# All instructions in the main block instead of a block per engine with an all-engine barrier at its end

## The chip, the cores and the metric

The kernel runs on one core of one Trainium2 chip. The trace shows five engines of the core, each with its own row of instructions: TensorE (PE in the profile), VectorE (DVE), ScalarE (ACT), GpSimd (POOL) and SyncE (SP). In this kernel they wait for one another through semaphores. For transfers between device memory and the core's on-chip memory the page gives each queue's share of 16 DMA engines; of the 83 issues in the trace of the kernel before, 81 are SP's and 2 ACT's.

The metric is the device time of one execution in microseconds (us). Each run also lists the core's *span*: from the first to the last recorded instruction of the program. The two are not the same (time less span was 1.25 to 1.88 us in the runs of this study), and the difference between them turns out to matter here.

## The reference, cut to what matters

```python
def reference(A_x, A_k_cache, A_v_cache, A_wq, A_wo, B_x, B_W_gate, B_W_up, B_W_down, gate_w):
    g = sigmoid((A_x * gate_w).sum(-1))
    a = attention(A_x, A_k_cache, A_v_cache, A_wq, A_wo)   # one token, 16 query heads,
                                                           # 8 key/value heads, 65536 keys of 256
    b = gated_mlp(A_x, B_W_gate, B_W_up, B_W_down)         # 448 -> 1792 -> 448
    return g * a + (1 - g) * b                             # (1, 1, 448)
```

The two caches are 8 x 65536 x 256 bfloat16 each, 268 MB. Every byte is used once for one token, so the work is reading memory: 549.03 MB by the page of the kernel before, at 428 GB/s over the span.

## The kernel before

The kernel collects its operations in a plan. Each operation has an engine, a sort key, a function that emits its instructions, and the operations that it depends on. `emit` writes one engine's operations in order, with a wait ahead of each where needed:

```python
    def emit(self, e, prog, eng):
        seen = {}
        for o in prog:
            need = {}
            for d in o.deps:
                k = ("d", d.dma) if d.dma is not None else ("e", d.eng)
                need[k] = max(need.get(k, 0), d.count)
            for k, v in need.items():
                if seen.get(k, 0) < v:
                    seen[k] = v
                    eng.wait_ge(self.dsem[k[1]] if k[0] == "d" else self.esem[k[1]], v)
            ins = o.fn(eng)
            ...                                   # increments the engine's or the DMA's semaphore
```

SP issues first the weights of the query projection, then the other weights and the K and V tiles of 8 MB, into a ring of three buffers. VectorE transposes each K tile, TensorE computes scores and later the weighted sum of V, ScalarE the exponentials. The end is a chain: last piece of V, TensorE, VectorE, TensorE's last projection, two copies, the output's transfer.

```python
        f0 = op("dv", T_END, lambda e: e.tensor_copy(fin_o[:, 0:D2], A_ps[0:1, 0:D2]), [fin])
        f1 = op("ac", T_END, lambda e: e.copy(fin_o[:, D2:D], A_ps[32:33, 0:D2]), [fin])
        f2 = dma("sp", T_END + 1, "out", lambda e: e.dma_start(out[0, :, :], fin_o), [f0, f1])
        ...
        progs = pl.finish()

        block = es.enter_context(nc.Block())

        @block.sync
        def _(e):
            pl.emit("sp", progs["sp"], e)
            e.wait_ge(pl.dsem["out"], 16)

        @block.tensor
        def _(e):
            pl.emit("pe", progs["pe"], e)
        ...                                       # vector, scalar, gpsimd alike
```

`nc.Block()` gives each engine a block of its own. The main block then ends with one branch per engine into these blocks, each of them ends with a branch to a common end, and at the common end stands an all-engine barrier: four engines drain (an instruction of that name, which by its record adds to a semaphore), GpSimd drains too, waits for all four and releases them. Another barrier of the same kind stands at the very start of the program, after four constants that GpSimd fills (MEMSETs from 0.24 to 0.43 us). It comes from the construction of the program and is in both kernels.

Of the kernel before, what the change touches and what calls it, by code (L numbers as in the profile page):

```python
# [90 lines left out]
def bass_gated_mix__gqa_block_cached__glu_gated_reglu__decode_kernel(  # L91
# [34 lines left out]
    es = ExitStack()  # L126
    with es:
# [62 lines left out]
        pl = _Plan(nc, es)  # L190
# [362 lines left out]
        pl.serialize(touch_m)  # L553
        progs = pl.finish()

        block = es.enter_context(nc.Block())

        @block.sync
        def _(e):
            pl.emit("sp", progs["sp"], e)  # L560
            e.wait_ge(pl.dsem["out"], 16)

        @block.tensor
        def _(e):
            pl.emit("pe", progs["pe"], e)

        @block.vector
        def _(e):
            pl.emit("dv", progs["dv"], e)

        @block.scalar
        def _(e):
            pl.emit("ac", progs["ac"], e)

        @block.gpsimd
        def _(e):
            pl.emit("gp", progs["gp"], e)

    return nc

# [27 lines left out]
```

## Time and profile before

| | before |
|---|---|
| time, median of 3 runs (range) | 1284.43 us (1284.39 to 1284.6) |
| span of the profiled run | 1283.3 us |
| moved from memory | 549.67 MB, mean 428 GB/s |
| busy: VectorE, TensorE | 49%, 33% |
| start of SP's first load | 0.72 us |
| start of the output's issue | 1281.73 us |

From the page of the kernel before: the span, the share of DMA time in 40 equal slices (a 9 is 90% or more), and the main queue (packets, MB, share of the 16 engines' span).

```profile
span 1283.3 us, 9919 instructions
...
DMA  9999999999999999999999999999999999999997
...
q1 hardware_dynamic: 12930, 549.03, 99.2%
```

Three stretches of the same run. The columns are: stretch, length, busy time of the five engines, granted clock, DMA share, GB/s.

```profile
0.00:40.00 40.00, 11.74 (x79) 8.95 (x80) 16.31 (x38) 1.86 (x3) 4.09 (x21) 0.81 0.96 403
40.00:1237.00 1197.00, 397.79 (x4319) 147.80 (x4323) 616.06 (x381) 59.33 (x112) 0.00 (x0) 0.62 1.00 433
1237.00:1283.30 46.30, 17.45 (x208) 6.15 (x200) 1.23 (x3) 0.34 (x1) 0.00 (x0) 0.68 0.82 335
```

The DMA engines are full for 1197 us. Nothing that the change touches happens there. What can be gained lies before the first load is issued and after the last bytes have landed. The beginning, from the timeline (start, duration, engine, line, operation; "q" marks an engine's sequencer):

```profile
0.33 0.10 POOL L593 MEMSET const-uint8-127<- 128x1 uint8 x1
0.72 0.51 ACTq L236 DMA_DIRECT2D P_sb<-in_A_x_dram  x1
0.72 0.39 SPq L407 DMA_DIRECT2D ring<-in_A_wq_dram  x1
0.78 0.06 DVE L239 MEMSET one_t<- 1x1 bf16 x1 [0.78 <-PEq L593]
```

The end, from the timeline, and then from the waits of SP's queue (who waited for whom, us in total, times, longest):

```profile
1281.31 0.38 DVE L549 CAST P_sb<-A_ps 1x224 bf16<-1x224 f32 x1 [1.51 <-PE A_ps L358]
1281.73 0.32 SPq L551 DMA_DIRECT2D out_dram<-P_sb  x1
```

```profile
SPq L127 <- DMA out_dram<-P_sb: 0.8, 1, 0.8
SPq L593 <- PEq L593: 0.7, 1, 0.7
SPq L127 <- PEq L127: 0.2, 1, 0.2
```

L127 is the line of the context that the block closes with. SP waits there for the output's landing and then, in the barrier, for the other engines.

### The profile page before, as it was taken

What the parts mean: (1) busy time and instruction counts of PE and PEld (TensorE: products, weight loads), DVE (VectorE), ACT (ScalarE), POOL (GpSimd) and SP (SyncE); (2) the same over time, 40 slices, a digit from 0 to 9 for tenths busy, and PEclk for the clock granted to TensorE, in tenths of its full rate; (3) what the DMA queues carried; (4) which work ended last, traced back from release to release, by engine and by line L of the source; (5) the groups of instructions that cost most, each with busy time, mean ns of one, the idle gap of its engine ahead of it and who ended that gap; (6) DMA issues with size and microseconds to landing.
All of it is one profiled execution on the core that took longest, in us unless ns stands there. A gap on an engine that the chain in (4) does not pass through costs nothing.

```text
span 1283.3 us, 9919 instructions
## 1 busy us (share of the span) xinstructions
PE 427.0 (33%) x4600; PEld 162.9 (13%) x4600; DVE 633.6 (49%) x421; ACT 61.5 (5%) x116; POOL 4.1 (0%) x21
## 2 busy tenths in 40 slices
PE   3633332334123432224331243321433323233235
PEld 2401110111001210001110111100111101011111
DVE  2597633465533655434555444555434555335600
ACT  0000000000000000000000000000000000000000
POOL 1000000000000000000000000000000000000000
PEclk8656666656666565667665666655666656666567
DMA  9999999999999999999999999999999999999997
GB/s 398 431 436 432 432 437 432 432 434 432 436 427 436 434 434 429 432 436 434 429 432 437 434 434 432 436 427 432 435 438 425 432 440 434 430 427 440 431 408 313
DMA packets 12975, 549.67 MB, mean 428 GB/s; under 512 B 1283, under 2 KB 3590, under 8 KB 3974
## 3 DMA queue, kind: packets, MB, share of 16 engines
q1 hardware_dynamic: 12930, 549.03, 99.2%
q8 instruction: 36, 0.59, 0.2%
q14 instruction: 5, 0.04, 0.0%
q10 hardware_dynamic: 4, 0.00, 0.0%
HBM read 549.03 MB, written 0.00 MB: 428 GB/s over the span
## 4 chain that ended last, share of the span: by engine, by line
DVE 34%; DMA 32%; another core or an unknown queue 16%; PE 15%; SPq 1%; ACT 1%; issue 1%
DVE ring L335 30%; DMA ring<-in_A_k_cache_dram 27%; PE ST L347 7%; PE O L378 6%; DMA ring<-in_B_W_up_dram 3%; DMA ring<-in_A_wo_dram 2%; DVE P_sb L480 1%; SPq L521 1%; DVE nmb L458 1%; PE PT L485 1%; PE M_ps L429 1%; PE M_ps L432 0%; ACT ptp L494 0%; DVE o_sb L389 0%
## 5 line engine op out<-in xcount | busy, mean ns | idle before, releaser
L335 DVE STREAM_TRANSPOSE ring<-ring 128x2048 uint32<-128x2048 uint32 x256 | 565.4, 2275 | 410.0 <-DMA ring<-in_A_k_cache_dram 410.0
L347 PE MATMUL ST<-ring,xm 128*16 128x512 bf16 x2048 | 224.2, 612 | 755.2 <-DVE ring L335 755.2
L347 PEld LDWEIGHTS ST<-ring,xm 128*16 128x16 bf16 x2048 | 61.9, 120 | 903.0 <-DVE ring L335 794.6
L378 PE MATMUL O<-ring,ptp 128*4 128x512 bf16 x2048 | 149.0, 453 | 34.3 <-DMA ring<-in_A_v_cache_dram 30.3
L460 ACT ACTIVATE P_sb<-ST,nmb 128x512 bf16<-128x512 f32 x32 | 45.3, 1414 | 1112.7 <-DVE nmb L458 1112.7
L458 DVE TENSOR_REDUCE nmb<-ST 128x1 f32<-128x512 f32 x32 | 22.0, 689 | 110.7 <-PE ST L347 110.7
L378 PEld LDWEIGHTS O<-ring,ptp 128*4 128x4 bf16 x2048 | 54.5, 99 | 128.5 <-issue 58.3
L389 DVE CAST o_sb<-O 128x512 bf16<-128x512 f32 x8 | 5.5, 692 | 80.5 <-PE O L378 80.5
L480 DVE TENSOR_TENSOR P_sb<-P_sb,hs 128x1024 bf16<-128x1024 bf16 x16 | 18.9, 1222 | 8.7 <-ACT hs L474 8.7
L485 PE MATMUL PT<-identb,P_sb 128*128 128x128 bf16 x128 | 16.6, 310 | 15.5 <-DVE P_sb L480 14.7
L429 PE MATMUL M_ps<-xT,ring 128*128 128x1 bf16 x84 | 9.4, 205 | 16.3 <-DMA ring<-in_B_W_up_dram 16.3
L485 PEld LDWEIGHTS PT<-identb,P_sb 128*128 128x128 bf16 x128 | 12.3, 140 | 18.3 <-DVE P_sb L480 18.3
L494 ACT COPY ptp<-PT 128x256 bf16<-128x256 bf16 x32 | 10.3, 375 | 23.0 <-PE PT L485 23.0
L307 PE MATMUL M_ps<-ring,P_sb 128*128 128x256 bf16 x64 | 10.1, 335 | 3.2 <-DMA ring<-in_A_wq_dram 3.2
L429 PEld LDWEIGHTS M_ps<-xT,ring 128*128 128x128 bf16 x84 | 7.2, 151 | 16.9 <-issue 16.5
L460 ACT ACTIVATION_READ_ACCUMULATOR P_sb<-ST,nmb 128x1 f32 x32 | 8.5, 267 | 0.0
L307 PEld LDWEIGHTS M_ps<-ring,P_sb 128*128 128x128 bf16 x64 | 7.6, 120 | 5.5 <-issue 3.3
L432 PE MATMUL M_ps<-xT,ring 128*64 128x1 bf16 x56 | 7.8, 276 | 0.0
L412 DVE STREAM_TRANSPOSE ptp<-P_sb 128x128 uint32<-128x128 uint32 x1 | 0.3, 313 | 13.5 <-ACT P_sb L411 13.5
L470 PE MATMUL M_ps<-identf,hs 128*2 128x128 f32 x8 | 2.6, 321 | 10.0 <-DVE hs L468 10.0
L432 PEld LDWEIGHTS M_ps<-xT,ring 128*64 128x64 bf16 x56 | 5.4, 191 | 0.4
L358 PE MATMUL A_ps<-ring,attnT 128*1 128x224 bf16 x64 | 4.6, 305 | 2.5 <-DMA ring<-in_A_wo_dram 2.5
(72 smaller groups left out, 60.1 us busy)
## 6 DMA issues: line engine op xcount, KB each, us to landing
ring<-in_A_v_cache_dram SPq DMA_DIRECT2D x1, 4096.0 KB, 29.3
ring<-in_A_wq_dram SPq DMA_DIRECT2D x1, 3072.0 KB, 10.2
ring<-in_A_wo_dram SPq DMA_DIRECT2D x1, 2240.0 KB, 31.8
ring<-in_A_v_cache_dram SPq DMA_DIRECT2D x1, 2048.0 KB, 23.6
ring<-in_B_W_down_dram SPq DMA_DIRECT2D x1, 1568.0 KB, 20.6
ring<-in_B_W_gate_dram SPq DMA_DIRECT2D x1, 1344.0 KB, 32.6
ring<-in_B_W_up_dram SPq DMA_DIRECT2D x1, 1344.0 KB, 35.3
ring<-in_A_v_cache_dram SPq DMA_DIRECT2D x1, 1024.0 KB, 25.6
```

What stands on the lines that cost most here:

```text
L307: ins = e.matmul(QN_ps, xw3[:, k_, 31 - j:159 - j], rhs, start=(j == 0 and kt == 0), stop=(j == J - 1 and kt == R3))
L335: return lambda e: e.transpose(v, v)
L347: ins = e.matmul(bank[32 * w:32 * w + 16, :], xm[:, x0:x0 + 16], ktv[sl][:, u0:u0 + 16, c, :, r_], start=(b == 0 and c == 0 and r_ == 0), ...
L378: ins = e.matmul(OP[h % 2][32 * g:32 * g + 4, :], ptp[h % 2][:, col:col + 13:4], ring[sl][:, k * 512:(k + 1) * 512], start=(a == 0 and k < ...
L429: e.matmul(GU_ps[:, c:c + 1], wf3[which][:, kt * F + ft:(kt + 1) * F:FT], xT[:, kt:kt + 1], start=(kt == 0), stop=False, skip_group_check= ...
L432: ins = e.matmul(GU_ps[64 * half:64 * half + 64, c:c + 1], wfh[which][:, ft:F // 2:FT], xT[:, R3 + half:R3 + half + 1], start=False, stop= ...
L458: smax[n] = op("dv", tk + 22, lambda e, n=n, NM=NM, t_=t_: e.tensor_reduce(NM[:, t_:t_ + 1], ST[n % 2][:], AX.X, ALU.max, negate=True), [q ...
L460: aexp[n] = op("ac", tk + 23, lambda e, n=n, t_=t_, NM=NM, RS=RS: e.activation(P_sb[:, t_:2048:4], ST[n % 2][:], ACTF.Exp, bias=NM[:, t_:t ...
L480: rsc = op("dv", tt, lambda e, X=X, pb=pb: e.tensor_tensor(pb, pb, X[:, 12:16].unsqueeze(1).to_broadcast([128, 256, 4]), ALU.mult), [h7, a ...
L485: ins = e.transpose(PT[rd][:, s * 128:(s + 1) * 128], P_sb[:, (rd * 8 + s) * 128:(rd * 8 + s + 1) * 128], identb[:, :])
L494: ins = e.copy(dst, src)
L521: dep = dma("sp", t, "vp%d" % i, lambda e, sl=sl, n=n, lo=lo, hi=hi: e.dma_start(ring[sl][:, lo * 256:hi * 256], v_src(n)[:, lo * 256:hi * ...
```

## The change

The intent is to save the branch into each engine's block at the start and the barrier at the end. Every engine's instructions are emitted into the main block; the waits between operations stay as they were.

```diff
-        block = es.enter_context(nc.Block())
-
-        @block.sync
-        def _(e):
-            pl.emit("sp", progs["sp"], e)
-            e.wait_ge(pl.dsem["out"], 16)
-
-        @block.tensor
-        def _(e):
-            pl.emit("pe", progs["pe"], e)
-        ...
+        pl.emit("ac", progs["ac"], nc.scalar)
+        pl.emit("sp", progs["sp"], nc.sync)
+        nc.sync.wait_ge(pl.dsem["out"], 16)
+        pl.emit("pe", progs["pe"], nc.tensor)
+        pl.emit("dv", progs["dv"], nc.vector)
+        pl.emit("gp", progs["gp"], nc.gpsimd)
```

More of the change, by code (lines that the diff above doesn't have):

```diff
@@ L554, in bass_gated_mix__gqa_block_cached__glu_gated_reglu__decode_kernel @@
         progs = pl.finish()
-        block = es.enter_context(nc.Block())
-        @block.sync
-        def _(e):
-            pl.emit("sp", progs["sp"], e)
-            e.wait_ge(pl.dsem["out"], 16)
-        @block.tensor
-        def _(e):
-            pl.emit("pe", progs["pe"], e)
-        @block.vector
-        def _(e):
-            pl.emit("dv", progs["dv"], e)
-        @block.scalar
-        def _(e):
-            pl.emit("ac", progs["ac"], e)
-        @block.gpsimd
-        def _(e):
-            pl.emit("gp", progs["gp"], e)
+        pl.emit("ac", progs["ac"], nc.scalar)
[4 more added lines that the diff above has]
+        pl.emit("gp", progs["gp"], nc.gpsimd)
     return nc
```

## The prediction

> **What bounds the kernel now.** The page's DMA row is 9 tenths in every slice but the last, and the queue table puts 99.2% of the 16 engines' span on the hardware queue. From 40 to 1237 us the DMA share is 1.00 at 433 GB/s; in the first 40 us it is 0.96 at 403 GB/s, in the last 46.3 us 0.82 at 335 GB/s. 549.67 MB at 433 GB/s are 1269 us (an estimate from those two numbers) of the 1283.3 us span. The time is the byte stream plus what precedes its first issue and follows its last landing; only those ends can be touched.
>
> **What the change removes.** No operation, transfer, or order within an engine.
> 1. Entry: one branch per engine. The timeline shows the last constant fill on POOL ending at about 0.43 us, the first SP issue at 0.72, the first ACT issue at 0.72, VectorE at 0.78, POOL at 0.82. The 0.3 us between hold the opening barrier, which stays, and the branch, which goes. [...]
> 2. Exit: the all-engine barrier. The output's issue starts at 1281.73 us and takes 0.32; the waits of SP show 0.8 us for the output's landing and then 0.2 us for TensorE's sequencer at the line of the block's exit. Landing is therefore at about 1282.85, and the span ends at 1283.3: 0.45 us are drain and barrier, on the critical path. In the changed kernel only SP's wait for the output is left.
>
> **What it adds or moves.** Nothing. The activation-table load (1.28 us at 1.50 us, on ACT behind its two small loads) could move ahead of those loads; their users have slack: xw is ready at 5.9 us, while the first projection waits for wq until 12.2 us. Should the table load land before the opening barrier, the whole program would start about 1.3 us later; unlikely, as it now stands just before its first user.
>
> **Sum.** [...] None of it is hidden; the run-to-run spread is 0.2 us. The DMA stream may lie a little differently, worth a few tenths to 1 us either way.
>
> Predicted 1283.9 us, 1282.3 to 1285.2 eight times in ten; faster by over 2%: 0.01, within 2%: 0.98, slower by over 2%: 0.01.
>
> **What would show it.** [...] Exit: the span ends at most 0.1 us after the output's landing instead of 0.45; no wait at the exit line for another engine's sequencer. Middle: DMA share 1.00 and 433 GB/s from 40 to 1237 us, K-tile transposes (17.7 us for eight) and busy times unchanged.
>
> **What would make it wrong.** The time measured may not contain the end barrier, or the closing work around the program may take its place [...]; a table load or instruction fetch that starts the stream later by 1 to 2 us; [...] a different memory rate of the stream.

The sum came to about 0.55 us (1284.43 less 0.55 is the 1283.9 us forecast). Of it 0.45 us are the exit; the rest was the entry. It was an estimate for a branch ahead of SP's first load, which was to start a little earlier than at 0.72 us; no trace showed what it rested on. That the stream may differ by a few tenths to 1 us was a guess; in one series of nine runs of the kernel before (that of the first experiments) the spans are 1282.0 to 1284.2 us.

## The result, and the profile after

| | before | after |
|---|---|---|
| time, median of 4 runs (range) | 1284.51 us (1284.39 to 1285.15) | 1284.11 us (1283.34 to 1284.89) |
| ratio of fast runs, 95% interval | | 0.9995 (0.9981 to 1.0009) |
| span of the profiled run | 1283.3 us | 1282.0 us |
| SP's first load | 0.72 us | 0.72 us |
| output's issue | 1281.73 us | 1280.89 us |
| from the output's issue to the end of the span | 1.53 us | 1.16 us |

A ratio is the mean time of one kernel's fast runs over that of the other's of the same rounds, so it is not quite the ratio of the medians. By this comparison the two are the same: 0.4 us between the medians, with single runs 1.5 us apart.

The page of the changed kernel, and its three stretches:

```profile
span 1282.0 us, 9908 instructions
...
DMA  9999999999999999999999999999999999999998
...
q1 hardware_dynamic: 12930, 549.03, 99.4%
```

```profile
0.00:40.00 40.00, 11.52 (x77) 8.74 (x77) 16.10 (x38) 1.86 (x3) 4.09 (x21) 0.82 0.96 403
40.00:1237.00 1197.00, 398.32 (x4317) 147.25 (x4321) 616.26 (x381) 59.33 (x112) 0.00 (x0) 0.61 1.00 433
1237.00:1282.00 45.00, 18.44 (x212) 6.27 (x204) 1.23 (x3) 0.34 (x1) 0.00 (x0) 0.65 0.85 348
```

The middle is the same to the last digit of rate. The start:

```profile
0.72 0.51 ACTq L236 DMA_DIRECT2D P_sb<-in_A_x_dram  x1
0.72 0.40 SPq L407 DMA_DIRECT2D ring<-in_A_wq_dram  x1
0.78 0.06 DVE L239 MEMSET one_t<- 1x1 bf16 x1 [0.78 <-PEq L577]
```

Nothing moved. The end, and the waits of SP:

```profile
1280.46 0.38 DVE L549 CAST P_sb<-A_ps 1x224 bf16<-1x224 f32 x1 [1.51 <-PE A_ps L358]
1280.89 0.32 SPq L551 DMA_DIRECT2D out_dram<-P_sb  x1
```

```profile
SPq L558 <- DMA out_dram<-P_sb: 0.8, 1, 0.8
SPq L577 <- PEq L577: 0.7, 1, 0.7
```

The wait for the other engines is gone, and the page counts 11 instructions fewer. Eleven is just the size of the barrier: a drain and a wait on four engines, a drain and two semaphore instructions on GpSimd. The ten branches of the kernel before are not in that number. The trace's own records, which also hold what the page does not count as busy, show only one of them: SP's closing branch, which carries the wait for the output. In the changed kernel that wait is an instruction of its own, so the count there is even. These are the records after the output's issue, in ns from its start (start, duration):

```
before:  SP branch, waits for the output      1139   33
         SP drain                             1312    7
         GpSimd waits for the four            1344   17
         GpSimd releases them                 1423   17
         SP released                          1464   17
         TensorE released                     1476   51     end of the span: 1527
after:   SP waits for the output              1141   17     end of the span: 1158
```

At the start, SP's first load begins 65 ns after the opening barrier has let SP go in the kernel before (release recorded 11721 to 11738, load at 11803) and 68 ns after it in the changed kernel (11907 to 11924, 11992). Between 65 and 68 ns there is no room left for a branch that takes time.

So the profile shows 0.37 us gained at the end of the span (1.53 less 1.16) and nothing at its start. The profiled spans differ by 1.2 us; the other 0.84 us is the output's issue coming earlier in that run. Whether that is chance or belongs to the kernel was the first question for experiments.

### The profile page after: what moved, and what is told of

It is laid out like the page before. It is cut to its first block, busy times and chain, and to the rows that moved or that the text cites. A ratio compares the mean times of both kernels' runs of the same rounds, so it can differ in the third digit from the quotient of the medians.

```text
span 1282.0 us, 9908 instructions
## 1 busy us (share of the span) xinstructions
PE 428.3 (33%) x4600; PEld 162.3 (13%) x4600; DVE 633.6 (49%) x421; ACT 61.5 (5%) x116; POOL 4.1 (0%) x21
## 4 chain that ended last, share of the span: by engine, by line
DVE 34%; DMA 32%; another core or an unknown queue 16%; PE 15%; SPq 1%; ACT 1%; issue 1%
DVE ring L335 30%; DMA ring<-in_A_k_cache_dram 27%; PE ST L347 7%; PE O L378 6%; DMA ring<-in_B_W_up_dram 3%; DMA ring<-in_A_wo_dram 2%; DVE P_sb L480 1%; SPq L521 1%; DVE nmb L458 1%; PE PT L485 1%; PE M_ps L429 1%; PE M_ps L432 0%; ACT ptp L494 0%; DVE o_sb L389 0%
## 5 line engine op out<-in xcount | busy, mean ns | idle before, releaser
L494 ACT COPY ptp<-PT 128x256 bf16<-128x256 bf16 x32 | 10.3, 375 | 23.0 <-PE PT L485 23.0
```

The costliest lines, as they stand in the source:

```text
L494: ins = e.copy(dst, src)
```

## The experiments

Two quantities are read from each run. The *tail* runs from the start of the output's issue to the end of the span, from the trace of the profiled run. What lies *outside* is a run's time less its span, which every run lists. All kernels computed the right result.

**The changed kernel, more rounds** (no edit).

> The changed kernel once more, with more rounds, to set its gain against the spread. Theory A (the closing barrier lies on the critical path and is all that was gained): 0.3 to 0.5 us under the kernel before, with an interval that may include 0, as single runs differ by 0.7 us or more. Rival B (the gain of the first comparison, 1.2 us in the profiled spans, is real and also comes from a stream that runs better in this kernel): 1 us or more under the kernel before, with an interval clear of 0. Rival C (nothing is gained): 0.0. Tail, from the start of the output's issue to the end of the span: 1.16 us, as in the first profile of it; before 1.53.

Measured: median 1283.95 us against 1285.00 us, ratio 0.9994 (0.9982 to 1.0007), tail 1.16 us. The means are 0.83 us apart (1284.94 and 1284.11), more than theory A's 0.3 to 0.5 and less than rival B's 1 us, with an interval that includes no difference. This decides nothing by itself.

**The barrier put back, without blocks.**

```diff
         pl.emit("gp", progs["gp"], nc.gpsimd)
+        nc.all_engine_barrier()
```

> The changed kernel with one all-engine barrier put back at its end, no branches. Theory A: the tail goes from 1.16 to about 1.5 us (before 1.53), first SP issue stays at 0.72 us, time within 0.2 us of the kernel before. Rival D (the branches into and out of the blocks are part of the gain): tail clearly under 1.5, say 1.35, [...].

Measured: median 1285.02 us, ratio 1.0002 (0.9989 to 1.0014), first load at 0.72 us, tail 1.41 us. The barrier accounts for 0.25 us of the 0.37 us. So theory A's 1.5 us was missed, and rival D is right about the exit and wrong about the entry. In the waits of SP the one for the other engines is back, behind the one for the output:

```profile
SPq L558 <- DMA out_dram<-P_sb: 0.8, 1, 0.8
...
SPq L563 <- PEq L563: 0.2, 1, 0.2
```

The missing 0.12 us stands in the records: here SP's drain begins 56 ns after the wait for the output (1140 to 1196), in the kernel before 173 ns after its branch (1139 to 1312). So with the closing branch, which is recorded, SP's next instruction comes 117 ns later.

**Blocks put back, without the barrier.**

```diff
+        for k, et, e in parts:                      # sp, pe, dv, ac, gp
+            nc.br("blk_" + k, engines=[et])
+        for k, et, e in parts:
+            with nc.body("blk_" + k, valid_engines=[et]):
+                pl.emit(k, progs[k], e)
+                if k == "sp":
+                    e.wait_ge(pl.dsem["out"], 16)
+                nc.br("fin", engines=[et])
+        nc.switch_bb("fin")
```

> The changed kernel with a block per engine put back, written with branches in and out, but no barrier at the end. Theory A: tail 1.16 to 1.2 us, first SP issue at 0.72 us; no record of an entry branch; time as the changed kernel (0.3 to 0.5 us under before). Rival D: [...] a tail of 1.3 us and more.

Measured: median 1284.66 us, ratio 0.9997 (0.9985 to 1.001), first load at 0.72 us, tail 1.17 us. Of ten branches only SP's last is recorded (33 ns, it carries the wait). The branches are 0.01 us of the tail when nothing follows them, as theory A expected. Barrier alone 0.25, closing branch alone 0.01, both 0.37 us: the 0.12 us is the branch ahead of a barrier.

**The barrier ahead of the wait for the output.**

```diff
-        nc.sync.wait_ge(pl.dsem["out"], 16)
         ...
         pl.emit("gp", progs["gp"], nc.gpsimd)
+        nc.all_engine_barrier()
+        nc.sync.wait_ge(pl.dsem["out"], 16)
```

> The changed kernel with the barrier put back, but ahead of SP's wait for the output instead of after it. Theory A says that the barrier costs because it begins after the landing; begun at the output's issue it runs under the 0.8 us of the landing: tail 1.16 to 1.2 us, time as the changed kernel. Rival E (the barrier's work costs wherever it stands, for instance through the longer end of each engine's program): tail about 1.5 us.

Measured: median 1283.94 us, ratio 0.9993 (0.998 to 1.0007), tail 1.15 us. The barrier is done 749 ns after the start of the output's issue, the landing comes at 1133 ns, and SP's waits show both side by side:

```profile
SPq L563 <- DMA out_dram<-P_sb: 0.4, 1, 0.4
SPq L562 <- PEq L562: 0.2, 1, 0.2
```

The barrier took the same 0.2 us of waiting, but out of the landing's time, so it added nothing to the span. Theory A's reason holds for the span, rival E falls.

**32 barriers at the end, and 32 at the start.**

```diff
+        for _ in range(32):                         # start32: here; end32: after the last emit
+            nc.all_engine_barrier()
         pl.emit("ac", progs["ac"], nc.scalar)
```

> 32 all-engine barriers at the end of the changed kernel. Theory A with 0.37 us for the first and somewhat less for those that follow (0.2 to 0.35 us each, a guess from the 0.36 us that drain, gather and release took in before): tail 8 to 12 us, and a time longer than the kernel before by 7 to 11 us, equal to the growth of the tail within 1 us. Rival C (the time measured does not contain the closing barrier): the tail grows in the trace but the time stays within 1 us of before.

> 32 all-engine barriers ahead of the program. If the head is on the critical path as the prediction said, SP's first issue moves from 0.72 us to 8 to 12 us, and the time grows by the same amount within 1 us. Rival F (the head has slack, the stream of bytes catches up): the first issue moves and the time grows by less than half of that.

Measured at the end: tail 12.34 us, which is 1.16 for the landing, 0.25 for the first barrier and (12.34 - 1.41) / 31 = 0.35 us for each further one, in all a little over the 8 to 12 us expected; time 1296.0 us median, mean 11.0 us over the kernel before, for a tail that is 10.8 us longer (12.34 against 1.53). Measured at the start: first load at 11.97 instead of 0.72 us, mean time 10.3 us over the kernel before. (The intervals, 1.007 to 1.0104 and 1.0065 to 1.0095, are clear of 1.)

```profile
11.97 0.38 SPq L407 DMA_DIRECT2D ring<-in_A_wq_dram  x1
```

Both ends pass into the time in full, so rivals C and F fall. There is no slack at the head: what delays the first load passes into the time. (The entry term of the prediction would be too little to see in the time, with runs of the kernel before 0.76 us apart; that the branches into the blocks cost nothing is read from the start of the first load.) What the start misses (11.25 us later, only 10.3 us longer) fits what is found further down: this kernel has no closing barrier, so it begins with an advantage of 0.9 us.

**Branches that really run.** In the first kernel, SP's first seven loads are put into a block each and laid out in reverse. In the second, only the first two stand behind the rest.

```diff
+        nc.br("sp0", engines=[ET.SP])               # taken8
+        for i in reversed(range(8)):
+            with nc.body("sp%d" % i, valid_engines=[ET.SP]):
+                if i < 7:
+                    pl.emit("sp", progs["sp"][i:i + 1], nc.sync)
+                    nc.br("sp%d" % (i + 1), engines=[ET.SP])
+                else: ...                           # the rest of SP's program
```

> SP's first seven loads each in a block of its own, the blocks laid out in reverse, so that eight branches between them cannot be left out by any layout. Tells what a taken branch costs that does run. [...] Time: within 1 us of before either way, as the queue already holds work by then.

Measured: median 1286.25 us, mean 1.13 us over the kernel before, a little outside the 1 us expected. All eight branches are recorded, 33 ns each, under the name COMPARE_BRANCH, which every recorded branch of this study has. The first load starts at 1.18 us instead of 0.72, 461 ns after the start of the branch that leads to it, and its issue takes 2.17 us instead of 0.40; the second starts at 3.56 us. The seventh starts 2.49 us later than in the changed kernel (6.35 against 3.86 us; the seven starts there are 0.72, 1.19, 1.65, 2.12, 2.83, 3.38 and 3.86), and nearly all of it comes from the first jump. From the third to the seventh load, four branches later, 2.26 us pass; in three profiles of the changed kernel 2.21, 2.26 and 2.13 us, and 2.06 us in that of end1, which has no branches either. The records show why so little is left: from the end of one issue to the start of the next 0.20 us pass with a branch between and 0.04 to 0.05 us without, so a short branch takes about 0.16 us of SP's time; but the issues themselves are shorter here, 0.33 to 0.43 us for the third to sixth against 0.42 to 0.67 us in the changed kernel. Together that is lost in the spread between profiles, while the first jump cost over 2 us (0.46 us in the start of the first load and 1.77 us in its issue).

> SP's first two loads laid out behind the rest of its program: one branch forward over 81 instructions, one back. In the run with eight such branches the first issue was 0.45 us late, the second waited 1.8 us longer, and the others came 0.07 us further apart than without branches. If the long waits come from a place that was not yet fetched: first issue about 0.45 us late and 1.5 to 2 us between the second load and the third. If they came from something else in that layout: all issues within 0.15 us of the changed kernel's.

Measured: median 1286.40 us, mean 1.21 us over the kernel before. SP's lines of the timeline:

```profile
1.18 2.10 SPq L407 DMA_DIRECT2D ring<-in_A_wq_dram  x1
3.33 0.41 SPq L408 DMA_DIRECT2D ring<-in_A_wq_dram  x1
4.05 0.32 SPq L452 DMA_DIRECT2D ring<-in_A_k_cache_dram  x1
```

The first issue is again 0.45 us late and again takes 2.1 us, here with a second load right behind it in the same block. The branch back to the third load, however, cost 0.26 us from its start (3.79) and not the 1.5 to 2 us expected. So the expectation was half right: the cost belongs to the first jump, not to each jump. (The first is also the only one among the loads that goes forward; the later ones there go back. The 0.07 us per branch that this text of expectations quotes from the run before is not borne out by the count above.)

The trace also records DMA packets of a kind that it calls "instruction". They would fit a fetch that holds up the long issue, but do not show it (in the changed kernel, SP's issue at 478.57 us lies inside the time of one of 16384 bytes and lasts only 0.33 us). In both kernels one such packet of 8192 bytes lies inside the long issue (from 1.74 us for 0.50 us, and from 1.73 us for 0.47 us); no other kernel has one in the first 6 us. In start32, ACT's first issue takes 1.94 us instead of 0.51 with two such packets inside it, and there is no branch at all. The trace does not say for which engine a packet is, and why SP's issue goes on for another 1.1 us after its packet stays open.

**A branch to a far place.** TensorE's last group of matmuls is laid out at the front of its program.

```diff
+        with nc.body("peb", valid_engines=[ET.PE]):
+            pl.emit("pe", progs["pe"][-1:], nc.tensor)
+            nc.br("fin", engines=[ET.PE])
+        with nc.body("pea", valid_engines=[ET.PE]):
+            pl.emit("pe", progs["pe"][:-1], nc.tensor)
+            nc.br("peb", engines=[ET.PE])
```

> TensorE's last group of projection matmuls (4 matmuls on the chain at the end) laid out at the front of its program, so that its last branch goes back over some 9000 instructions. Tells what a branch to a far place costs. If it stalls for a fetch, TensorE's last four matmuls start 1 to 3 us later after the ones before them than in the changed kernel (there 0.16 us after), and the time grows by 1 to 3 us less what the wait for the last projection weights covers. If not, under 0.2 us.

Measured: median 1288.12 us, mean 2.6 us over the kernel before (one of the four runs, 1285.95 us, was 2 us under the rest). The trace records the branch back with a duration of 3.27 us, from 1281.26 us; its beginning lies under matmuls that still run, and in the chain that ended last 2.71 us of it show as "issue", time in which TensorE waited for nothing that the profile shows:

```profile
1280.68 1.30 PE A_ps L358 x12
1281.98 2.71 issue
1284.70 0.55 PE A_ps L358 x4
```

The last four matmuls begin 3.12 us after the start of the one before them, in the changed kernel 0.23 us (not the 0.16 us of the expectation): 2.9 us later, within the 1 to 3 us expected of a fetch (a guess). The profiles' pages count the packets of the queue that they call "instruction", 16384 bytes each, first of the kernel before, then of this one:

```profile
q8 instruction: 36, 0.59, 0.2%
q8 instruction: 38, 0.62, 0.2%
```

One of the two packets more runs from 1282.22 to 1283.18 us, within the branch, the other from 1285.29 us, after TensorE's last branch to the end. So a branch can be dear: this one, with its target some 9000 instructions back, took 2.7 us on the critical chain, with an instruction packet of 0.96 us inside it. None of the ten in the kernel before is of this kind.

**The surplus, once more** (all three are kernels shown above; no new edit).

> The changed kernel a third time, on whatever chip this is, to separate two readings of the 0.5 to 0.8 us by which its means lay under the kernel before so far. Theory A: the tail is 0.37 us shorter and the rest, the time of the output's issue, differs by chance: mean 0.37 us under before, give or take 0.4, and no steady order among these kernels except by tail. Rival B (the stream itself runs better in this kernel, by about 0.8 us): mean 1.2 us under before.

> The kernel with one barrier put back, again. Its tail was 1.41 us, its mean 0.15 us over before. Theory A: mean 0.12 us under before, give or take 0.4, and 0.25 us over the changed kernel. Rival B: 0.8 to 1 us over the changed kernel, as in the first runs.

> The kernel with the barrier ahead of the wait, again. Its tail was 1.15 us, its mean 1.0 us under before and 1.2 us under the kernel with the barrier at the end, while the tails explain 0.38 and 0.26. Theory A (the surplus was chance): 0.38 us under before and 0.26 us under the kernel with the barrier at the end, give or take 0.4. Rival B: again 1 us and 1.2 us.

Measured, on another chip: changed kernel median 1284.14 us, ratio 0.9992 (0.9979 to 1.0004), mean 1.08 us under the kernel before. Barrier at the end: 1285.23 us, ratio 0.9999, mean 0.16 us under. Barrier ahead of the wait: 1284.07 us, ratio 0.9992, mean 1.00 us under. The two groups of the first series came back (barrier last, and not last), and the surplus with them. Theory A as stated is too small, and chance is no longer a good answer. But rival B's reason is wrong as well. The table takes the mean time of each kernel apart: the output's issue is the mean span less the tail, and outside is the mean of time less span.

| kernel | chip | runs | mean time | output's issue | tail | outside |
|---|---|---|---|---|---|---|
| before | first | 9 | 1284.94 | 1281.62 | 1.53 | 1.80 |
| after_again | first | 5 | 1284.11 | 1281.66 | 1.16 | 1.29 |
| branch_only | first | 5 | 1284.53 | 1281.97 | 1.17 | 1.39 |
| bar_then_wait | first | 5 | 1283.91 | 1281.35 | 1.15 | 1.41 |
| end1 | first | 5 | 1285.10 | 1281.85 | 1.41 | 1.84 |
| before | third | 9 | 1285.25 | 1281.92 | 1.53 | 1.81 |
| after3 | third | 5 | 1284.18 | 1281.71 | 1.15 | 1.32 |
| btw_b | third | 5 | 1284.25 | 1281.68 | 1.16 | 1.41 |
| end1_b | third | 5 | 1285.10 | 1281.87 | 1.41 | 1.82 |
| before | second | 7 | 1285.09 | 1281.79 | 1.53 | 1.78 |
| end32 | second | 4 | 1296.14 | 1282.04 | 12.34 | 1.76 |
| start32 | second | 4 | 1295.43 | 1292.97 | 1.15 | 1.31 |

(The tail of before is that of its one profile. Spans are on record to 0.1 us, so one run's outside is good to 0.05 us.) The stream of bytes runs alike: the output's issue of the changed kernel lies 0.04 us later on one chip and 0.21 us earlier on the other, and kernels without a steady reason differ by as much. Rival B falls: its 0.8 us are not there on either chip. What differs steadily stands in the last column: every kernel whose last act is a barrier has 1.76 to 1.84 us outside its span, every other one 1.29 to 1.41 us (the three kernels with jumping branches, which are not in the table, 1.38 to 1.45 us). Over all 25 runs of before it is 1.74 to 1.86, over all 14 runs of the changed kernel 1.25 to 1.35 us, so the two do not even touch. Within the second group a closing branch or a barrier ahead of the wait goes with some 0.1 us more outside than the changed kernel has (1.39 and 1.41 against 1.29 to 1.32).

The last column goes with how the engines end. With a barrier as the last act, which holds all five until the end, it is 1.76 to 1.84; in bar_then_wait the other four engines are let go 0.4 us before SP ends, and it is 1.41; in branch_only SP ends with its one recorded branch, 1.39; with nothing behind the wait, 1.3. This was seen after the last run and was not put to a test of its own. Shown is that the 0.5 us belong to a barrier in the last place; what fills them is in no trace.

No version came out that beats the changed kernel: bar_then_wait lies within its spread (0.20 us under it on one chip, 0.07 us over it on the other).

## Why the prediction was right

It forecast 1283.9 us (1282.3 to 1285.2) and "within 2%" at 0.98; measured were 1284.11 us and 0.9995. The total was right, the sum behind it only in part. How near it came is partly luck: the forecast gain was 0.55 us, the means of the first comparison differ by 0.53, but the parts measured below add up to 0.86, made of one term that was absent, one too large and one left out. The range of 2.9 us would also have held the unchanged kernel's 1284.51 us.

- *The stream of bytes is the bound and the change does not touch it.* Right: DMA share 1.00 at 433 GB/s from 40 to 1237 us in both, the output's issue alike on both chips.
- *Entry, a branch less ahead of SP's first load.* Wrong. SP's first load starts at 0.72 us in both and within 3 ns of the same distance from the barrier. The failed step is the assumption that a branch written into the program is one that runs: nine of the ten leave no record, and with the blocks put back the load still starts at 0.72 us. That they are left out because their target is the next instruction of that engine anyway is the likely reading, since branches do appear as soon as the target is moved elsewhere (all eight of SP's in taken8). So the entry term had no object here.
- *Exit, 0.45 us of drain and barrier.* Right in kind, a little too large: the tail became 0.37 us shorter. Of this 0.25 us is the barrier, and 0.12 us the one branch that does run, ahead of it. The prediction counted that branch with the barrier; only the two experiments that put back one part each told them apart. The size was off since it was taken from rounded figures, 1282.85 and 1283.3 us; the records have SP's wait for the landing over at 1282.87 and the end of the span at 1283.26, and 0.02 us of SP's wait remain in the changed kernel.
- *None of it is hidden.* Right, and shown both ways: 32 barriers lengthen the time by what they last at either end, and a barrier under the output's landing adds nothing to the span (tail 1.15 against 1.16 us).
- *The risk that the closing work around the program takes the barrier's place, so that the exit gains nothing.* The reverse happened. The time outside the span got 0.5 us shorter, and this term was missing in the sum. With it the expected gain is 0.37 + 0.49 = 0.86 us (0.49 is 1.80 less the 1.31 of the changed kernel's 14 runs). The means of the three comparisons show 0.53 (1284.64 less 1284.11), 0.83 and 1.08 us.
- *A table load or a fetch that starts the stream later.* Did not happen: the first load starts at 0.72 us in both, the table load (1.28 us) at 1.50 and 1.51 us. First issues of about 2 us appear only in kernels of the experiments, two whose branches were made to jump (2.17 us in taken8, 2.10 us in taken2) and start32 (ACT's, 1.94 us), and an "issue" gap of 2.71 us on the closing chain only in far.

## What to carry to other kernels

A block per engine cost here its closing barrier, and little else: nine of the ten branches left no record and delayed nothing (SP's first load 65 ns after the opening barrier with them, 68 ns without), so there was nothing to save in them. A barrier as the program's last act cost twice, once in the span and once more outside it, together with its branch 0.86 us; that is not to be seen in 1284 us, though it would be some 4% of a kernel of 20 us (an estimate from the 0.86 us here). Where the expected gain is below the run-to-run spread, read the two ends of the trace and the time less the span rather than the time, and multiply the suspect by 32 to see whether it passes into the time at all.
